# The written order of phase one of an mLSTM plus two MoE layers: gates earlier, R and the table switches moved, x copied at its transposes

## The chip, the cores and the metric

One core of a Trainium2 chip runs the whole program. The metric is the device time of one execution in microseconds (us). The kernel before takes 656.52 us, the median of three runs (656.23 to 657.03). Engines are called by the names that the profile uses: PE multiplies matrices, PEld loads their weights, DVE, ACT and POOL work on tiles elementwise, SP issues DMAs. Every engine takes its own instructions in the order in which they are written, and waits where an operand isn't there yet.

## What is computed

The input is an attention with gates (an mLSTM) for 2 batches, 8 heads, 768 positions and head size 40; its output x (1536 rows of 320) goes through a mixture of 4 experts and then through a gated layer of width 1536.

```python
m_new = maximum(f + m, i);  f_stab = exp(f + m - m_new);  i_stab = exp(i - m_new)
C = f_stab * C + i_stab * outer(v, k);   n = f_stab * n + i_stab * k
y[t] = sigmoid(o) * (C @ q) / maximum(abs(n @ q), 1)
# x: (1536, 320)
out += p[:, e] * (relu(x @ w1[e]) @ w2[e])        # e = 0..3
result = ((x2 @ w_a) * (x2 @ w_b)) @ w_out
```

## The kernel before

The attention is done in chunks of 128 positions: tile n is chunk j = n // 2 of batch n % 2, twelve tiles in all. In a chunk the product of q and k (`scores`, L411) is multiplied with a matrix of decays. That matrix is the exponential of a matmul of two tiles that the gates give: LT and Rr, the R of the title (`weights_of`, L402: PE, then ACT's exp, then a mask on POOL at L409). What comes before the chunk is held in a state cbd (`state`, L479).

Every matrix product with the experts' weights is done in two parts, a rounded high one and the rest: a weight piece is loaded by SP (L84), cast by ACT (wh, L88) and subtracted by POOL or DVE (wl, L90; `LOENG`, L34, says which engine). The same is done to x (`split_hi`, `split_lo`: xh by ACT at L130, xl by DVE at L133 and the rest of the third block by DVE at L135).

Phase one runs until 207 us. Its 72 **items** (`Item`, L203) are the first three half experts, 256 columns of x at a time: part a is 8 matmuls into psa (L201), a ReLU by ACT (hh, L218) and a subtraction by DVE (hl, L219), and part b, two items later, 6 matmuls into psy (L242 to L244). psa has two buffers, and so has psy in pairs. After items 7 and 11 of a round ACT or DVE takes psy away (`add_expert`, L251 and L253). Twelve items are a **round**; round r computes with the x of chunk r, and beside them runs the attention of chunk r + 1.

What of the attention stands where is written out by hand: `ev` (L622 to L650) is a list of (item, function, arguments), sorted by its first number, and the loop at L670 calls whatever is due before an item, in the middle of it (up to k + 0.5, between its part a and the part b that follows), and after it (up to k + 0.99). So the list is the order of every engine's queue. For chunks 2 to 5 the numbers are relative to the first item of the round (t0).

Names that the steps below touch: `gate1` to `gate4` and `gate_tail` (L331 to L393) go from a chunk's gates to LT (L368), zx (L367), exponentials and ET; `build_R` (L395) makes Rr from zx, on DVE for the first four tiles and on POOL afterwards; `split_qk` (L293) splits q and k (ACT L301, DVE L304); `s1b` (L423) multiplies scores and decays (DVE L425); `s2a` (L427) is the matmuls with v and with the state (PE L435, L441); `s2b` (L444) is seven small DVE steps from there to x (L451 to L464), closed by a copy by ACT of the last 64 columns of x (L465); `s3a` (L495) is three PE transposes of x, of which the third reads that copy; `s3b` splits their result. `table` (L525) makes ACT load the table of Exp or of Sigmoid, `o_gate` is the sigmoid (L315), `weights` (L528) the experts' weights pg, `weigh_k` (POOL L474) weighs k for the state. The tiles of PSUM that the attention uses (pt_...) come from one pool of four buffers, in the order in which they are asked for.

Of the kernel before, what the change touches and what calls it, by code (L numbers as in the profile page):

```python
# [7 lines left out]
F32 = mybir.dt.float32  # L8
# [5 lines left out]
AF = mybir.ActivationFunctionType  # L14
# [3 lines left out]
DM = H * D  # L18
# [12 lines left out]
NI = 12  # L31
NF = 2
NP = 4
LOENG = {0: "ppvppppp", 1: "pppppppp", 2: "pppppppp", 3: "vpvpvpvp", 4: "vpvpvpvp", 5: "vpvpvpvp"}  # L34
RB = 3
QB = 3
QENG = ("vector", "vector")
# [9 lines left out]
def mlstm_moe_kernel(ctx, tc, gates, qk, qc, kvo, dp, w1b, w2b, ident_d, bdmask_d, rsel_d, exp_d, out):  # L47
# [145 lines left out]
    def mm_group(ps, wh, wl, o0, c, o, n):  # L193
        k = lambda w, t: w[:, o0 + t * P:o0 + (t + 1) * P]
        x = lambda t, i: t[c][:, i, o:o + n]
        prs = [
            (k(wh, 0), x(xh, 0)), (k(wh, 1), x(xh, 1)), (k(wh, 2), x(xh, 2)), (k(wl, 0), x(xh, 0)),
            (k(wl, 1), x(xh, 1)), (k(wl, 2), x(xh, 2)), (k(wh, 0), x(xl, 0)), (k(wh, 1), x(xl, 1)),
        ]
        for i, (l, r) in enumerate(prs):  # L200
            nc.tensor.matmul(ps, l, r, start=(i == 0), stop=(i == len(prs) - 1))  # L201
# [59 lines left out]
    with ExitStack() as c1:  # L261
# [101 lines left out]
        def gate3(j):  # L363
            g = g_sb[j]
            zh, L, cm = g["zh"], g["L"], g["cm"]
            zx = a2.tile([64, P], F32R, tag="zx", name="zx")
            nc.vector.scalar_tensor_tensor(zx, zh[0:64].bitcast(F32), rsel[0:64, 16:17], L[0:64], op0=ALU.mult, op1=ALU.add)  # L367
            nc.vector.scalar_tensor_tensor(LT[j % 2][64:G], zh[64:G].bitcast(F32), rsel[64:G, 16:17], cm[64:G], op0=ALU.mult, op1=ALU.add)  # L368
            g["zx"] = zx

        def gate4(j):
# [72 lines left out]
        def s2b(n):  # L444
            j, b = n // 2, n % 2
            t = td[n]
            r = og[j][:, b].rearrange("p (h d) -> p h d", d=D)
            y = a2.tile([P, H, DE], F32, tag="y", name="y_t", bufs=1)
            pyv = t["py"][:, 0:H * DE].rearrange("p (h e) -> p h e", e=DE)
            if j > 0:  # L450
                nc.vector.tensor_tensor(  # L451
                    y, t["pi"][:, 0:H * DE].rearrange("p (h e) -> p h e", e=DE),
                    g_sb[j]["ET"][:, b * H:(b + 1) * H].unsqueeze(2).to_broadcast([P, H, DE]), op=ALU.mult)
                nc.vector.tensor_tensor(y, pyv, y, op=ALU.add)
            else:
                y = pyv
            dn = a2.tile([P, H, 1], F32, tag="dn", name="dn_t")
            nc.vector.tensor_scalar(dn, y[:, :, D:DE], -1.0, 1.0, op0=ALU.mult, op1=ALU.max)
            nc.vector.tensor_tensor(dn, y[:, :, D:DE], dn, op=ALU.max)
            nc.vector.reciprocal(dn, dn)  # L460
            x = a2.tile([P, DM + 64], F32, tag="x", name="x_t")
            xv = x[:, :DM].rearrange("p (h d) -> p h d", d=D)
            nc.vector.tensor_tensor(xv, y[:, :, 0:D], dn.to_broadcast([P, H, D]), op=ALU.mult)
            t["last"] = nc.vector.tensor_tensor(xv, xv, r, op=ALU.mult).ins  # L464
            nc.scalar.copy(x[:, DM:], x[:, 256:DM])  # L465
            t["x"] = x

        def weigh_k(n):
# [74 lines left out]
        load_kvo(1)  # L543
        load_qk(0, 0)
        load_qk(0, 1)
        load_qk(1, 0, nc.scalar)
        load_qk(1, 1, nc.scalar)
        for t in LT:
            nc.vector.memset(t[0:64].bitcast(F32), 1.0)
        nc.sync.dma_start(td[0]["kvo"][:, NK:NK + NV], kvo[0, :, NK:NK + NV])  # L550
        load_o(0, nc.sync)
        nc.sync.dma_start(td[1]["kvo"][:, NK:NK + NV], kvo[1, :, NK:NK + NV])
        nc.sync.dma_start(ident, ident_d)
        go(w0[:4])
# [30 lines left out]
        load_kvo(2)  # L585
        load_qk(3, 0)
        load_qk(3, 1)
        load_kvo(3)
        load_o(1, nc.sync)
        o_gate(0)  # L590
        for n in range(2):
            s1b(n, 0)
            s1b(n, 1)
        go(w0[:2])
        go(w0[:2])
        s2a(0, 0)
        s2a(0, 1)
# [15 lines left out]
        split_hi(td[1]["pv"], 0, P)  # L613
        split_lo(td[1]["pv"], 0, P)
        warm_up(1)
        go(w0[5:7])
        go(w0[4:7])
        gate1(1, V)
        load_gates(2)
        go(w1[2:6])  # L620

        ev = [  # L622
            (0.5, gate2, 1), (0.5, gate_hi, 1, nc.vector.tensor_copy), (0.5, table, AF.Exp), (0.6, go, w0[7:]), (0.7, go, w0[7:]), (0.8, go, w1[6:]), (0.9, gate_tail, 0), (0.95, weigh_k, 0),
            (1.5, gate3, 1), (1.5, build_R, 2, V, 0, 4), (1.5, weigh_k, 1), (1.6, gate4, 1), (1.8, go, w1[0:2]), (1.9, go, w1[0:2]), (1.9, state, 0),
            (2.5, build_R, 2, V, 4, 8), (2.5, state, 1), (2.7, go, w2[:2]), (2.8, gate_tail, 1), (2.8, go, w1[2:4]), (2.9, go, w1[2:4]), (2.9, scores, 2, 0),
            (3.5, scores, 2, 1), (3.5, build_R, 3, V, 0, 4), (3.8, go, w1[4:6]), (3.9, weights_of, 2, 0), (3.9, go, w1[4:6]), (3.9, go, w2[2:4]),
            (4.5, weights_of, 2, 1), (4.5, build_R, 3, V, 4, 8), (4.6, table, AF.Sigmoid), (4.7, go, w1[6:8]), (4.8, s1b, 2, 0), (4.8, go, w1[6:8]), (4.9, o_gate, 1), (4.9, go, w2[4:6]),
            (5.3, table, AF.Exp), (5.4, s1b, 2, 1), (5.5, s2a, 2, 0), (5.6, s2a, 2, 1), (5.8, go, w2[0:2]), (5.9, s2b, 2), (5.9, scores, 3, 0), (5.9, weights_of, 3, 0), (5.9, go, w2[6:8]), (5.9, go, w2[0:2]),
            (6.0, weigh_k, 2), (6.8, go, w2[2:4]), (6.9, s1b, 3, 0), (6.9, go, w2[2:4]),
            (7.0, scores, 3, 1), (7.0, weights_of, 3, 1), (7.2, weights), (7.4, s3a, 2), (7.5, weigh_k, 3), (7.7, go, w2[4:6]), (7.9, s1b, 3, 1), (7.9, s3b, 2), (7.9, go, w2[4:6]),  # L630
            (8.5, s2a, 3, 0), (8.6, s2a, 3, 1), (8.7, go, w2[6:8]), (8.9, s2b, 3), (8.9, go, w2[6:8]),
            (9.4, state, 2), (9.9, state, 3), (10.6, s3a, 3), (10.9, s3b, 3),
        ]
        for j in range(2, NCH):
            n0, n1, t0 = 2 * j, 2 * j + 1, NI * (j - 1)
            new = [
                (-6.4, load_kvo, n0), (-6.2, load_o, j, nc.sync), (-5.4, load_kvo, n1),
                (-4.4, load_qk, n0, 0), (-3.4, load_qk, n0, 1), (-2.4, load_qk, n1, 0), (-1.4, load_qk, n1, 1),
                (-8.4, gate1, j, V), (-5.8, gate2, j), (-5.1, gate_hi, j, nc.scalar.copy), (-3.6, gate3, j), (-3.4, gate4, j), (-3.1, build_R, n0, nc.gpsimd), (-2.0, build_R, n1, nc.gpsimd), (-1.1, gate_tail, j),
                (-1.5, split_qk, n0, 0), (-0.5, split_qk, n0, 1),  # L640
                (0.5, s1a, n0, 0), (1.5, s1a, n0, 1), (1.6, split_qk, n1, 0),
                (2.0, table, AF.Sigmoid), (2.4, s1b, n0, 0), (2.5, o_gate, j), (2.6, split_qk, n1, 1), (2.9, table, AF.Exp),
                (3.4, s1b, n0, 1), (3.5, s1a, n1, 0), (3.6, weigh_k, n0),
                (4.2, s2a, n0, 0), (4.5, s2a, n0, 1), (4.6, weigh_k, n1), (4.95, s2b, n0),
                (5.4, s1b, n1, 0), (6.2, s1a, n1, 1), (6.9, state, n0), (7.2, s3a, n0), (7.4, s1b, n1, 1), (7.6, state, n1), (7.9, s3b, n0),
                (8.2, s2a, n1, 0), (8.5, s2a, n1, 1), (8.95, s2b, n1), (10.6, s3a, n1), (10.9, s3b, n1),
            ]
# [188 lines left out]
```

## Time and profile before

| | us |
|---|---|
| time, median of 3 runs | 656.52 |
| the profiled execution: its time / its span | 656.55 / 654.8 |
| start, until the first item (0 to 19.25) | 19.25 |
| round 0 (19.25 to 71.85) | 52.60 |
| rounds 1, 2, 3 | 34.96, 34.95, 34.58 |
| round 4 | 31.15 |
| round 5 and all that follows (207.49 to the end) | 447.31 |
| busy over the span: PE, PEld, DVE, ACT, POOL | 630.3, 572.5, 429.3, 264.2, 181.3 |

The profile is of one execution whose own time is 656.55 us. A round is measured from the first matmul of its first item to that of the next round. "Busy" of PE is the time that the records of matmuls cover. Round 5 has no attention left beside it.

### The profile page before, as it was taken

Reading aid. Unit: us, or ns where it says so; the run is one execution under the profiler, and the core shown is the slowest. Engines: PE = TensorE matmul, PEld = TensorE weight load, DVE = VectorE, ACT = ScalarE, POOL = GpSimd, SP = SyncE. Lnnn points to the kernel's source line nnn. Section 1 sums busy time; section 2 is a strip of 40 time slices with the busy share of each in tenths; the row PEclk is TensorE's granted clock in tenths of the full one; section 3 lists DMA queues with packets and bytes.
Section 4 is the critical chain, followed back from the end, with each engine's and each line's share of the span. In section 5 each row is a group of like instructions: output and inputs, shape, how many; then the busy total and the mean of one; then the engine's idle time right before and its main releaser. Section 6 shows DMA issues by size and latency. Waiting matters only on the chain.

```text
span 654.8 us, 10289 instructions
## 1 busy us (share of the span) xinstructions
PE 630.3 (96%) x3798; PEld 572.5 (87%) x3799; DVE 429.3 (66%) x858; ACT 264.2 (40%) x592; POOL 181.3 (28%) x219
## 2 busy tenths in 40 slices
PE   8796999999899999999999999999999999999997
PEld 6686998989899988989888988898888888888886
DVE  7859687878665233433478888898765767764343
ACT  5563635445453322323343444354644433332221
POOL 3557351332310111233233333332121212220000
PEclk9799899999999999999999999999999999999999
DMA  7944216161600212222221222121111111000003
GB/s 217 253 144 107 61 54 163 55 163 55 155 12 23 68 45 59 74 62 72 80 69 52 72 66 69 52 69 53 35 36 34 53 34 52 18 0 2 1 10 111
DMA packets 27487, 45.99 MB, mean 70 GB/s; under 512 B 3189, under 2 KB 17773, under 8 KB 27437
## 3 DMA queue, kind: packets, MB, share of 16 engines
q1 hardware_dynamic: 27337, 45.00, 24.9%
q8 instruction: 30, 0.49, 0.3%
q10 hardware_dynamic: 100, 0.33, 0.2%
q14 instruction: 20, 0.16, 0.1%
HBM read 43.35 MB, written 1.97 MB: 69 GB/s over the span
## 4 chain that ended last, share of the span: by engine, by line
PE 80%; DVE 9%; ACT 4%; issue 4%; POOL 2%; DMA 1%; ACTq 0%; POOLq 0%; DVEq 0%
PE psa L201 33%; PE psy L242 11%; PE psy L244 10%; PE psy L243 10%; PE psb L201 10%; PE pt_y L435 1%; DVE LT L368 1%; ACT qs_t L301 1%; DMA acc<-in_w1b 1%; POOL wl L90 1%; PE pt_c L417 1%; DVE qs_t L304 1%; ACT L526 1%; ACT hh L218 1%; PE pt_i L441 1%
## 5 line engine op out<-in xcount | busy, mean ns | idle before, releaser
L242 PE MATMUL psy<-wh,hh 128*128 128x320 f32 x528 | 167.1, 317 | 9.2 <-ACT acc L251 9.1
L244 PE MATMUL psy<-wh,hl 128*128 128x320 f32 x528 | 163.7, 310 | 0.0
L243 PE MATMUL psy<-wl,hh 128*128 128x320 f32 x528 | 163.6, 310 | 0.0
L219 DVE SCALAR_TENSOR_TENSOR hl<-psa,hh 128x256 fp32r<-128x256 f32 (+1 forms) x132 | 71.9, 544 | 120.2 <-ACT hh L218 119.6
L201 PE MATMUL psa<-xh,wh 128*128 128x512 f32 (+1 forms) x504 | 122.5, 351 | 0.8 <-DVE xh L135 0.4
L218 ACT ACTIVATE hh<-psa 128x256 fp32r<-128x256 f32 (+1 forms) x132 | 62.8, 478 | 147.1 <-PE psa L201 147.1
L201 PE MATMUL psa<-xh,wl 128*128 128x512 f32 (+1 forms) x504 | 120.2, 347 | 0.0
L242 PEld LDWEIGHTS psy<-wh,hh 128*128 128x128 f32 x528 | 99.9, 189 | 16.3 <-ACT acc L251 10.2
L243 PEld LDWEIGHTS psy<-wl,hh 128*128 128x128 f32 x528 | 100.0, 189 | 4.0
L244 PEld LDWEIGHTS psy<-wh,hl 128*128 128x128 f32 x528 | 99.7, 189 | 0.0
L201 PEld LDWEIGHTS psa<-xh,wl 128*128 128x128 f32 x504 | 85.4, 190 | 12.6
L201 PEld LDWEIGHTS psa<-xh,wh 128*128 128x128 f32 x504 | 84.6, 190 | 9.0 <-DVE xh L135 0.9
L201 PE MATMUL psa<-xl,wh 128*128 128x512 f32 (+1 forms) x336 | 89.6, 348 | 0.0
L122 POOL TENSOR_TENSOR wl<-tp,lf 128x272 fp32r<-128x272 f32 x48 | 38.7, 807 | 124.3 <-DVE tp L121 124.3
L201 PEld LDWEIGHTS psa<-xl,wh 128*128 128x128 f32 x336 | 58.8, 190 | 8.2
L228 DVE TENSOR_TENSOR g<-psa,bs 128x512 f32<-128x512 f32 x36 | 24.9, 691 | 50.4 <-PE psa L201 50.4
L119 POOL TENSOR_TENSOR lf<-lf,sq 128x272 f32<-128x272 f32 x48 | 37.2, 775 | 70.3 <-ACT wh L118 39.5
L90 POOL TENSOR_TENSOR wl<-raw,wh 128x352 fp32r<-128x352 f32 x28 | 26.4, 950 | 96.9 <-ACT wh L88 84.3
L229 ACT CAST hh<-g 128x512 fp32r<-128x512 f32 x36 | 22.3, 620 | 72.4 <-DVE g L228 72.4
L409 POOL TENSOR_SCALAR_AFFINE_SELECT w_t<-w_t 128x512 f32<-128x512 f32 x24 | 15.2, 639 | 96.6 <-ACT w_t L408 90.6
L230 DVE TENSOR_TENSOR hl<-g,hh 128x512 fp32r<-128x512 f32 x36 | 24.9, 692 | 24.7 <-ACT hh L229 24.7
L224 ACT COPY bs<-psb 128x512 f32<-128x512 f32 x36 | 21.1, 587 | 44.0 <-PE psb L201 43.9
(118 smaller groups left out, 896.0 us busy)
## 6 DMA issues: line engine op xcount, KB each, us to landing
raw<-in_w2b SPq DMA_DIRECT2D x48, 272.0 KB, 2.7
qk_t<-in_qk SPq DMA_DIRECT2D x16, 480.0 KB, 6.3
raw<-in_w1b SPq DMA_DIRECT2D x40, 176.0 KB, 2.3
acc<-in_w1b SPq DMA_DIRECT2D x24, 176.0 KB, 3.6
kvo_t<-in_kvo SPq DMA_DIRECT2D x10, 364.5 KB, 4.4
og_t<-in_kvo SPq DMA_DIRECT2D x6, 320.0 KB, 3.0
out<-acc SPq DMA_DIRECT2D x12, 160.0 KB, 1.8
qc_t<-in_qc SPq DMA_DIRECT2D x10, 180.0 KB, 3.1
```

The source lines that it names most:

```text
L90: lo_eng.tensor_tensor(wl[:, cs], raw, wh[:, cs].bitcast(F32), op=ALU.subtract)
L119: nc.gpsimd.tensor_tensor(lf, lf, sq, op=ALU.mult)
L122: nc.gpsimd.tensor_tensor(wl[:, cs], tf, lf, op=ALU.add)
L201: nc.tensor.matmul(ps, l, r, start=(i == 0), stop=(i == len(prs) - 1))
L218: nc.scalar.activation(self.hh, ps, AF.Relu)
L219: nc.vector.scalar_tensor_tensor(self.hl, ps, 0.0, self.hh.bitcast(F32), op0=ALU.max, op1=ALU.subtract)
L228: nc.vector.tensor_tensor(g, ps, bs, op=ALU.mult)
L229: nc.scalar.copy(self.hh, g)
L230: nc.vector.tensor_tensor(self.hl, g, self.hh.bitcast(F32), op=ALU.subtract)
L242: nc.tensor.matmul(ps, lh, wh[:, off:off + DM], start=(fi == 0), stop=False)
L243: nc.tensor.matmul(ps, lh, wl[:, off:off + DM], start=False, stop=False)
L244: nc.tensor.matmul(ps, ll, wh[:, off:off + DM], start=False, stop=(fi == nf - 1))
```

## The change

The order of phase one is rewritten; nothing is computed otherwise.

- `gate1` to `gate4` and both `build_R` of chunks 3 to 5 stand 2 to 3.8 items sooner, so that `build_R` comes at items 6.25 and 8.0 of the round before instead of 8.9 and 10.0; those of chunk 2 are written out in the list of round 0, 1 to 2.8 items later than they were. In `gate3` LT is made ahead of zx.
- ACT's copy of x moves from the end of `s2b` to the start of `s3a`.
- Sigmoid, with its two table loads, moves from items 2.0 to 2.9 of a chunk's own round to items 8.0 to 9.5 of the round before.
- In round 0 the first two states and their `weigh_k` move from items 0.95 to 2.5 to items 2.5 to 5.45, `weights` from 7.2 to 3.2, and the pieces of the third half expert come up to 1.3 items sooner. Two more pieces of the first half expert are subtracted on DVE.
- The eight matmuls of part a take the products with the third block of x last.
- Loads: tile 1's q and k are issued by SP instead of ACT, the first two pieces ahead of o, tile 3's kvo in round 0; kvo has three buffers instead of four, and the second kvo of a chunk is loaded 3.4 items later, the next gates 2.3 items sooner.
- At the start the casts of the first two pieces stand ahead of the sigmoid.

The diff, without its unchanged lines:

```diff
-LOENG = {0: "ppvppppp", 1: "pppppppp", 2: "pppppppp", 3: "vpvpvpvp", 4: "vpvpvpvp", 5: "vpvpvpvp"}
+LOENG = {0: "ppvpvpvp", 1: "pppppppp", 2: "pppppppp", 3: "vpvpvpvp", 4: "vpvpvpvp", 5: "vpvpvpvp"}
...
-            (k(wh, 0), x(xh, 0)), (k(wh, 1), x(xh, 1)), (k(wh, 2), x(xh, 2)), (k(wl, 0), x(xh, 0)),
-            (k(wl, 1), x(xh, 1)), (k(wl, 2), x(xh, 2)), (k(wh, 0), x(xl, 0)), (k(wh, 1), x(xl, 1)),
+            (k(wh, 0), x(xh, 0)), (k(wh, 1), x(xh, 1)), (k(wl, 0), x(xh, 0)), (k(wl, 1), x(xh, 1)),
+            (k(wh, 0), x(xl, 0)), (k(wh, 1), x(xl, 1)), (k(wh, 2), x(xh, 2)), (k(wl, 2), x(xh, 2)),
...
-            t["kvo"] = a2.tile([P, NK + NV], F32, tag="kvo", name="kvo_t", bufs=4)
+            t["kvo"] = a2.tile([P, NK + NV], F32, tag="kvo", name="kvo_t", bufs=3)
...
+            nc.vector.scalar_tensor_tensor(LT[j % 2][64:G], zh[64:G].bitcast(F32), rsel[64:G, 16:17], cm[64:G], op0=ALU.mult, op1=ALU.add)
-            nc.vector.scalar_tensor_tensor(LT[j % 2][64:G], zh[64:G].bitcast(F32), rsel[64:G, 16:17], cm[64:G], op0=ALU.mult, op1=ALU.add)
...
-            nc.scalar.copy(x[:, DM:], x[:, 256:DM])
...
+            nc.scalar.copy(x[:, DM:], x[:, 256:DM])
...
-        load_qk(1, 0, nc.scalar)
-        load_qk(1, 1, nc.scalar)
+        load_qk(1, 0)
+        load_qk(1, 1)
+        nc.sync.dma_start(td[1]["kvo"][:, NK:NK + NV], kvo[1, :, NK:NK + NV])
+        go(w0[:2])
-        nc.sync.dma_start(td[1]["kvo"][:, NK:NK + NV], kvo[1, :, NK:NK + NV])
-        go(w0[:4])
+        go(w0[2:4])
...
-        load_kvo(3)
+        go(w0[:2])
-        go(w0[:2])
...
+        go(w0[4:5])
-        go(w0[4:7])
+        go(w0[5:6])
-            (0.5, gate2, 1), (0.5, gate_hi, 1, nc.vector.tensor_copy), (0.5, table, AF.Exp), (0.6, go, w0[7:]), (0.7, go, w0[7:]), (0.8, go, w1[6:]), (0.9, gate_tail, 0), (0.95, weigh_k, 0),
-            (1.5, gate3, 1), (1.5, build_R, 2, V, 0, 4), (1.5, weigh_k, 1), (1.6, gate4, 1), (1.8, go, w1[0:2]), (1.9, go, w1[0:2]), (1.9, state, 0),
-            (2.5, build_R, 2, V, 4, 8), (2.5, state, 1), (2.7, go, w2[:2]), (2.8, gate_tail, 1), (2.8, go, w1[2:4]), (2.9, go, w1[2:4]), (2.9, scores, 2, 0),
-            (3.5, scores, 2, 1), (3.5, build_R, 3, V, 0, 4), (3.8, go, w1[4:6]), (3.9, weights_of, 2, 0), (3.9, go, w1[4:6]), (3.9, go, w2[2:4]),
+            (0.5, gate2, 1), (0.5, gate_hi, 1, nc.vector.tensor_copy), (0.5, table, AF.Exp), (0.6, go, w0[7:]), (0.7, go, w0[6:]), (0.8, go, w1[6:]), (0.9, gate_tail, 0),
+            (1.5, gate3, 1), (1.5, build_R, 2, V, 0, 4), (1.6, gate4, 1), (1.8, go, w1[0:2]), (1.9, go, w1[0:2]),
+            (2.5, build_R, 2, V, 4, 8), (2.5, weigh_k, 0), (2.7, go, w2[:2]), (2.8, gate_tail, 1), (2.8, go, w1[2:4]), (2.9, go, w1[2:4]), (2.9, scores, 2, 0),
+            (3.0, weigh_k, 1), (3.2, weights), (3.5, scores, 2, 1), (3.5, build_R, 3, V, 0, 4), (3.8, go, w1[4:6]), (3.9, weights_of, 2, 0), (3.9, go, w1[4:6]), (3.9, go, w2[2:4]),
-            (5.3, table, AF.Exp), (5.4, s1b, 2, 1), (5.5, s2a, 2, 0), (5.6, s2a, 2, 1), (5.8, go, w2[0:2]), (5.9, s2b, 2), (5.9, scores, 3, 0), (5.9, weights_of, 3, 0), (5.9, go, w2[6:8]), (5.9, go, w2[0:2]),
-            (6.0, weigh_k, 2), (6.8, go, w2[2:4]), (6.9, s1b, 3, 0), (6.9, go, w2[2:4]),
-            (7.0, scores, 3, 1), (7.0, weights_of, 3, 1), (7.2, weights), (7.4, s3a, 2), (7.5, weigh_k, 3), (7.7, go, w2[4:6]), (7.9, s1b, 3, 1), (7.9, s3b, 2), (7.9, go, w2[4:6]),
-            (8.5, s2a, 3, 0), (8.6, s2a, 3, 1), (8.7, go, w2[6:8]), (8.9, s2b, 3), (8.9, go, w2[6:8]),
-            (9.4, state, 2), (9.9, state, 3), (10.6, s3a, 3), (10.9, s3b, 3),
+            (5.0, state, 0), (5.2, go, w2[0:2]), (5.3, table, AF.Exp), (5.4, s1b, 2, 1), (5.4, go, w2[0:2]), (5.45, state, 1), (5.45, load_kvo, 3), (5.5, s2a, 2, 0), (5.6, s2a, 2, 1), (5.9, s2b, 2), (5.9, scores, 3, 0), (5.9, weights_of, 3, 0), (5.9, go, w2[6:8]), (5.95, go, w2[2:4]),
+            (6.0, weigh_k, 2), (6.1, go, w2[2:4]), (6.4, gate1, 2, V), (6.6, go, w2[4:6]), (6.8, go, w2[4:6]), (6.9, s1b, 3, 0),
+            (7.0, scores, 3, 1), (7.0, weights_of, 3, 1), (7.4, s3a, 2), (7.4, go, w2[6:8]), (7.45, gate2, 2), (7.5, weigh_k, 3), (7.6, go, w2[6:8]), (7.9, s1b, 3, 1), (7.9, s3b, 2),
+            (8.3, gate_hi, 2, nc.scalar.copy), (8.5, s2a, 3, 0), (8.6, s2a, 3, 1), (8.9, s2b, 3),
+            (9.4, state, 2), (9.5, gate3, 2), (9.9, state, 3), (10.0, build_R, 4, nc.gpsimd), (10.2, gate4, 2), (10.6, s3a, 3), (10.9, s3b, 3), (10.9, gate_tail, 2), (11.0, build_R, 5, nc.gpsimd),
-                (-6.4, load_kvo, n0), (-6.2, load_o, j, nc.sync), (-5.4, load_kvo, n1),
+                (-6.4, load_kvo, n0), (-6.2, load_o, j, nc.sync), (-2.0, load_kvo, n1),
-                (-8.4, gate1, j, V), (-5.8, gate2, j), (-5.1, gate_hi, j, nc.scalar.copy), (-3.6, gate3, j), (-3.4, gate4, j), (-3.1, build_R, n0, nc.gpsimd), (-2.0, build_R, n1, nc.gpsimd), (-1.1, gate_tail, j),
+                (-4.0, table, AF.Sigmoid), (-3.5, o_gate, j), (-2.5, table, AF.Exp),
-                (2.0, table, AF.Sigmoid), (2.4, s1b, n0, 0), (2.5, o_gate, j), (2.6, split_qk, n1, 1), (2.9, table, AF.Exp),
+                (2.4, s1b, n0, 0), (2.6, split_qk, n1, 1),
+            if j > 2:
+                new += [
+                    (-11.4, gate1, j, V), (-8.4, gate2, j), (-7.7, gate_hi, j, nc.scalar.copy), (-7.4, gate3, j), (-6.0, gate4, j),
+                    (-5.75, build_R, n0, nc.gpsimd), (-4.0, build_R, n1, nc.gpsimd), (-1.1, gate_tail, j),
+                ]
-                new += [(0.1, load_gates, j + 1)]
+                new += [(-2.2, load_gates, j + 1)]
```

## Rows read from the trace of the kernel before

**Rows 1.** Stages: length, busy us of PE, PEld, DVE, ACT, POOL, clock, DMA, GB/s.
```profile
19.25:71.85 52.60, 42.37 (x281) 40.19 (x282) 39.28 (x71) 25.49 (x63) 32.89 (x36) 0.87 0.55 150
71.85:106.81 34.96, 33.10 (x259) 32.40 (x259) 27.30 (x55) 16.23 (x39) 11.81 (x13) 1.00 0.34 90
...
207.49:654.80 447.31, 442.69 (x2426) 394.56 (x2424) 274.25 (x544) 162.14 (x365) 102.36 (x124) 1.00 0.18 50
```

**Rows 2.** PE's waits over the whole run: total us, times, longest us.
```profile
PE psy L242 <- ACT acc L251: 9.1, 4, 4.4
PE pt_u L486 <- POOL kw_t L474: 3.3, 1, 3.3
PE pt_y L435 <- DVE w_t L425: 3.0, 6, 1.0
...
PE pt_y L435 <- ACT warm L526: 0.6, 1, 0.6
PE psb L201 <- DVE xh L135: 0.6, 1, 0.6
```

**Rows 3.** The two stretches after PE's long waits, columns as in rows 1.
```profile
25.48:30.90 5.42, 5.42 (x25) 5.42 (x26) 5.29 (x10) 1.00 (x3) 2.63 (x4) 0.50 0.91 251
...
64.72:72.00 7.28, 7.28 (x31) 6.95 (x32) 4.98 (x9) 3.67 (x8) 5.33 (x4) 0.53 0.26 69
```

**Rows 4.** Timeline around 24 us: start, us, engine, line, out<-in, [idle before <-releaser].
```profile
22.89 0.42 DVE L219 SCALAR_TENSOR_TENSOR hl<-psa,hh 128x256 fp32r<-128x256 f32 x1
23.94 0.31 ACT L375 ACTIVATE ex<-L 64x128 f32<-64x128 f32 x1
...
25.48 1.58 PE L486 MATMUL pt_u<-kvo_t,kw_t 128*120 128x123 f32 x6 [3.27 <-POOL kw_t L474]
```

**Rows 5.** Timeline around 60 us.
```profile
56.34 4.58 DVE L368 SCALAR_TENSOR_TENSOR LT<-zh,rsel,cm 48x128 fp32r<-48x128 f32 x1
62.02 0.17 DVE L458 TENSOR_SCALAR dn_t<-y_t 128x8 f32<-128x8 f32 x1
63.72 0.24 ACT L465 COPY x_t<-x_t 128x64 f32<-128x64 f32 x1 [8.83 <-DVE x_t L464]
64.72 0.41 PE L242 MATMUL psy<-wh,hh 128*128 128x320 f32 x1 [4.42 <-ACT acc L251]
```

**Rows 6.** Timeline of ACT and PE at the end of round 2, items 9 to 11.
```profile
137.04 0.94 ACT L251 ACTIVATE acc<-psy,pg 128x320 f32<-128x320 f32 x2
137.86 0.39 ACT L218 ACTIVATE hh<-psa 128x256 fp32r<-128x256 f32 x1
138.13 1.06 ACT L301 CAST qs_t<-qk_t 120x1024 fp32r<-120x1024 f32 x1
139.14 0.48 ACT L130 CAST xh<-pt_x 128x384 fp32r<-128x384 f32 x1
...
133.84 0.40 PE L201 MATMUL psa<-xl,wh 128*128 128x256 f32 x2
...
135.68 0.40 PE L201 MATMUL psa<-xl,wh 128*128 128x256 f32 x2
137.62 0.41 PE L242 MATMUL psy<-wh,hh 128*128 128x320 f32 x1 [1.54 <-ACT acc L251]
```

**Rows 7.** Timeline of ACT in round 3: a table load and the next ReLU.
```profile
150.60 1.28 ACT L526 ACT_TABLE_LOAD   x1
...
152.00 0.36 ACT L218 ACTIVATE hh<-psa 128x256 fp32r<-128x256 f32 x1
```

**Rows 8.** Timeline of DVE and POOL at the end of round 1: R beside s2b.
```profile
98.39 0.50 DVE L451 TENSOR_TENSOR y_t<-pt_i,ET 128x328 f32<-128x328 f32 x1
...
99.46 0.69 DVE L458 TENSOR_SCALAR dn_t<-y_t 128x8 f32<-128x8 f32 x1
...
96.32 3.79 POOL L398 TENSOR_TENSOR Rr<-zx,rsel 64x1024 fp32r<-64x1024 f32 x2
```

**Rows 9.** A group of round 0 by line: count, busy us, mean ns, idle before.
```profile
L90 POOL TENSOR_TENSOR wl<-acc,wh 128x352 fp32r<-128x352 f32 x20 | 19.5, 994 | 6.4 <-ACT wh L88 6.4
```

## The prediction

> **What bounds the kernel now.** I read the stages first. From 207.49 us on PE is busy 442.69 of 447.31 us, and the change reaches that part only through the order of eight matmuls. Round 1 takes 34.96 us with PE busy all but 2, and rounds 2 to 4 are no longer. Round 0 does the same kind of work in 52.60 us [rows 1]: that is the stage to look at.
>
> The second view is what PE waits for [rows 2]. Three lines carry it. 9.1 us go to L251, which takes psy away; 3.3 us to the weighed k of the first state; 3.0 and 0.6 us to `s2a`, whose decays come late. They sum to 16.0 us.
>
> The third view is PE's clock. After the wait of 3.27 us [rows 4] PE works 5.42 us at 0.50, and after the one of 4.42 us [rows 5] 7.28 us at 0.53 [rows 3]; otherwise it is at full speed in phase one. At half speed half of the time is lost: 5.42 x 0.5 = 2.7 us and 7.28 x (1 - 0.53) = 3.4 us. So waits and clock together cost 16.0 + 6.1 = 22.1 us, and that is nearly all that a better order can bring.
>
> **Part by part, what is removed.**
>
> *The first states.* PE reaches `state(0)` 3.27 us before POOL has weighed k [rows 4]. At item 5 k is long weighed. The wait goes, and the half clock behind it: 3.3 + 2.7 = 6.0 us.
>
> *The copy of x, and LT.* L465 waits in ACT's queue for the end of `s2b` on DVE: 8.83 us in round 0. The ReLU and L251, whose inputs were there, stand behind it, and PE stands behind L251 for 4.42 us [rows 5]. In rounds 1 to 3 it is the same at some 1.5 us each (1.54 in round 2 [rows 6]; all four together 9.1 [rows 2]). In round 0 DVE is late because LT, a step on 48 x 128 elements, took 4.58 us [rows 5], beside POOL at work; with LT ahead of zx, R can't start before it. At `s3a` x is ready, so these waits go: 9.1 + 3.4 = 12.5 us.
>
> *Sigmoid.* The two table loads of 1.28 us [rows 7] stand, in a chunk's own round, ahead of ReLUs on which the decays' last product (L425) waits. That and the late masks of round 0 make the 3.0 + 0.6 us at `s2a` [rows 2]. Away from there the wait goes: 3.6 us.
>
> **What is added.**
>
> *The copy at the transposes.* Now the third transpose waits for a copy that is issued right before it, behind whatever ACT holds. For the first tile of a chunk `s3a` stands in the middle of an item, directly behind part a, so ACT has that item's ReLU (0.36 [rows 7]) and the copy (0.24 [rows 5]) to do, and PE the two other transposes, about 0.2: with the handoffs 0.5 us of waiting, once a round, 2.0 us in rounds 1 to 4. Below, it is nothing if ACT is ahead; above, a cast of 1.06 [rows 6] in the way makes it 1.6 a round. For the second tile, in the three rounds 1 to 3, `split_qk`'s cast (1.06) stands ahead too. In round 2 the cast ended where L130 began, 139.14 [rows 6].
>
> *The Exp table at item 9.5.* It now stands right ahead of L251. Take round 2. Part a of item 9 ended at 134.2, that of item 10 at 136.1 [rows 6]. With ACT free the ReLU of item 9 begins at 134.3 and the table load at 134.7; from the start of a load to the next ReLU it takes 1.40 us [rows 7], so L251 begins at 136.1 and its first copy ends at 136.6. PE is there at 135.9 (the start of its last two, 135.68, and 0.2): 0.74 us instead of 1.54. Then ReLU 136.9, cast 137.2 to 138.2, copy to 138.45; the third transpose can start at 138.5 and was due at 137.75: another 0.75. So PE waits 1.49 us where it waited 1.54, in each of three rounds: 2.2 + 2.25 = 4.5 us. Bounds: nothing if ACT gets there early, and double if one more cast of 1.06 is late.
>
> With the 2.0 us of the first tiles this is 6.5 us, against 4.7 us at L251 (9.1 less 4.4 [rows 2]) and, by my split of the 3.0, 1.5 us at `s2a` that these rounds lose today: **rounds 1 to 4 gain nothing.**
>
> The Trainium skill, "TensorE: Matmul & The Clock Gate", Architectural detail, says that ACT and DVE are strict first in, first out, and that of PE's queue only weight loads are pulled ahead. That speaks against this part of the change. If PE could run part b past the waiting transpose, the sum would be some 4 us lower, by the transposes' terms; nothing in these rows shows it doing so.
>
> *R and the gates earlier.* Per round, nothing is added. R on POOL (3.79 us for two [rows 8]) slows DVE steps whose inputs all lie in SBUF: L458 takes 0.69 us beside it, 0.17 alone [rows 5, 8]. L451, which reads PSUM, takes its 0.50 beside it. At item 6.25 DVE has hl, L425 and the state's product to do, all of PSUM; at 8.0 R should be over before `s2b`. If it isn't, 0.5 us of DVE per step, covered by the items until `s3a` at 10.6: 0. The Trainium skill, "SBUF — State Buffer", Who interferes with whom, has this as a rule: a DVE instruction with two SBUF inputs and a POOL one that reads SBUF exclude each other. By it, the two pieces moved to DVE in round 0 could each wait for one of POOL's, 0.99 us [rows 9], and the sum would be 2 us higher if none of that were covered.
>
> *Round 0's new waits.* PE's gap no longer hides DVE. hl of item 0 ends at 23.3, after gate1 [rows 4], while PE would want its buffer at 22.2; an added piece on DVE and less of POOL beside gate1 cancel: 0.5 us by my count, 0 to 1.1. `gate_tail(1)` wants ACT's exponentials, which began at 23.94 [rows 4] and have a table load, a cast and two ReLUs ahead: 0.9. The two states now ask for PSUM buffers that `s1b` of tile 2 must free, behind POOL's masks, and these behind pieces of 0.99 us each [rows 9]: 1.6 (0 to 3). `s3a` of tile 2: 0.6 for the copy, and its buffer waits for another `s1b`: 0.5 to 2.2 in all, and I take 1.0, near the lower end, since the longest wait of PE for L425 today is 1.0 [rows 2]. `s3a` of tile 3, behind exponentials and the cast: 1.3. Sum 5.3, of which 0.3 comes back as the third block's products come last (0.4 us of PE's wait at the first item was for L135): **5.0**, with 1 and 11 as ends.
>
> *The rest.* Third block last in the later phase: half of the 0.6 us at psb [rows 2], -0.3. The casts ahead of the first sigmoid give POOL its first pieces sooner, and o's DMA comes later; x of tile 0 has its sigmoid at about the same time: 0, within 0.5. Tile 1's q and k go through SP about 1 us later, with the decays' chain ahead of their use: 0. kvo with three buffers, and the loads that stand behind it on SP: each waits for a state that PE does at least two items earlier: 0. Moving tile 3's kvo out of a stretch with DMA at 0.91 [rows 3] brings the pieces behind it forward; nothing waits on them once POOL is the later one: 0. `weights` at 3.2: four DVE steps in the shadow of PE: 0.
>
> **The sum**, against the profiled execution's 656.55 us, which is within 0.03 of the median: 656.55 - 22.1 + 5.0 + 6.5 - 0.3 = 645.65, **645.7 us**. By its own terms this case spans 641 to 650 (round 0's added waits 1 to 9).
>
> **Rivals.**
>
> *ACT is never in the way.* If ACT keeps ahead at item 9.5 and at the transposes, 6.5 us and 1.9 of round 0's fall away: 637.3, 634 to 640. For it: ACT is busy only 16.2 of 35 us in a round [rows 1]. Against: in-order queues, and the casts right there.
>
> *The waits of round 0 meet.* If POOL's masks and the states come one behind the other in one wait of over 3 us, the clock falls as it did after 3.27 us [rows 3, 4] and takes some 3 us more: 645.7 + 3 + 3 = 652. For it: POOL has 32.9 us of work in round 0 [rows 1], which must now fit in some 41. It decides from 3 us in one piece; waits of 1.5 us did no harm.
>
> *ACT is the new bound: slower.* The place is items 9 to 11. If at each copy the whole queue lies ahead (L251 twice 0.94, ReLU, cast 1.06, table 1.4, copy 0.24: 4.0 us against my 1.5), four rounds lose 10 us more, and the five copies behind an exponential of 0.6 us more, 3: 645.7 + 13 = 659. It decides from 10.9 us beyond my added 11.5. For it: one L465 holds ACT for 8.83 us today [rows 5]. Against: ACT's inputs are ready this time.
>
> *It does nothing.* All that goes comes back in the same rounds: 656. For it: in rounds 1 to 4 that is my own reckoning; but the two long waits of round 0 have no successor of that length.
>
> **How the numbers follow.** My forecast has 0.56, ACT out of the way 0.18, the meeting waits 0.17, slower 0.06, nothing 0.03. The first three are all faster by more than 0.2%, 1.3 us, which is about what a measurement of this kernel can tell from no change: faster 0.91, within 0.2% 0.03, slower 0.06. The range takes in the first three: 635 to 652.
>
> **What would show it.** Right: round 0 is 41 to 43 us long, with the clock at 1.00 and no wait of PE over 2 us; L465 disappears from ACT's waits; LT takes 0.35 us everywhere; the third transpose waits for ACT in every chunk; PE still waits for L251 by 0.5 to 1 us in rounds 1 to 3, whose lengths stay within 0.5 us of before. Wrong: rounds 1 to 3 at 33 us (ACT was ahead), a stretch at half clock (the waits met), or a PE wait on SP's loads, which I have costed at nothing.

## The result and the profile after

The changed kernel takes 647.60 us (median of 4, 646.99 to 648.15) beside 656.77 for the kernel before in the same comparison: a ratio of 0.9848, 95% interval 0.9811 to 0.9886. Its profiled execution takes 647.9 us with a span of 646.2, that of before 656.55 and 654.8.

The stages of after, by the first matmul of each round as in [rows 1] and in its columns: start, rounds 0, 1 and 4, and the rest.

```profile
0.00:18.11 18.11, 15.70 (x90) 11.21 (x91) 14.85 (x38) 11.84 (x22) 8.34 (x17) 1.00 0.81 232
18.11:64.77 46.66, 38.64 (x282) 36.78 (x282) 37.82 (x72) 28.91 (x68) 32.26 (x34) 0.93 0.66 184
64.77:99.50 34.73, 33.26 (x259) 32.23 (x258) 24.46 (x55) 17.04 (x39) 12.17 (x13) 1.00 0.32 79
...
168.09:199.12 31.03, 30.64 (x241) 30.08 (x240) 19.14 (x44) 11.96 (x27) 3.02 (x4) 1.00 0.14 39
199.12:646.20 447.08, 442.75 (x2426) 394.53 (x2424) 274.34 (x544) 162.28 (x365) 102.83 (x124) 1.00 0.17 50
```

One boundary of before has to be put right for the comparison. Its round 4 begins at 175.90 us and not at 176.34, which is the third matmul of that item, so its rounds 3 and 4 take 34.14 and 31.59 us and not 34.58 and 31.15. PE of before, and the two stages:

```profile
175.90 0.40 PE L201 MATMUL psa<-xh,wh 128*128 128x256 f32 x2
...
176.34 0.39 PE L201 MATMUL psa<-xh,wh 128*128 128x256 f32 x1
...
141.76:175.90 34.14, 32.16 (x254) 31.61 (x253) 26.09 (x54) 16.75 (x38) 11.58 (x12) 1.00 0.39 103
175.90:207.49 31.59, 31.05 (x240) 30.30 (x239) 19.78 (x46) 14.83 (x32) 2.54 (x4) 1.00 0.14 37
```

Against the kernel before the start is 1.14 us shorter, round 0 5.94, rounds 1 to 4 0.23, 0.22, 0.28 and 0.56, the rest 0.23: 8.6 us in all. So round 0 carries the gain, as forecast, but it is 46.66 us long where I expected 41 to 43, and its clock is 0.93.

PE's waits of after, columns as in [rows 2]:

```profile
PE pt_x L140 <- ACT x_t L496: 4.7, 9, 1.2
PE pt_e L389 <- POOL eb L380: 2.8, 1, 2.8
PE psy L242 <- ACT acc L251: 1.7, 3, 0.6
...
PE psa L201 <- DVE hl L219: 1.3, 1, 1.3
PE pt_y L435 <- DVE w_t L425: 1.3, 1, 1.3
PE pt_y L435 <- issue: 1.0, 1, 1.0
PE psb L201 <- DVE xh L135: 0.6, 1, 0.6
```

L251 fell from 9.1 to 1.7 us, and the wait for the weighed k is gone. New are the third transpose (L140) and one that I hadn't foreseen, 2.8 us for eb. The timeline around it, POOL and then PE, and three stretches in the columns of [rows 1], the first two within the wait and the third with the work behind it:

```profile
57.10 2.35 POOL L398 TENSOR_TENSOR Rr<-zx,rsel 64x1024 fp32r<-64x1024 f32 x1
59.41 0.63 POOL L380 TENSOR_TENSOR eb<-expd,ex 16x2 f32<-16x2 f32 x1
...
56.88 0.33 PE L140 MATMUL pt_x<-ident,x_t 128*128 128x128 f32 x1 [1.21 <-ACT x_t L496]
57.04 0.25 PE L386 MATMUL pt_e<-ident,ex 96*128 96x96 f32 x1
60.09 1.15 PE L389 MATMUL pt_e<-eb,expd 16*120 16x2 f32 x5 [2.81 <-POOL eb L380]
...
57.50:58.00 0.50, 0.00 (x0) 0.00 (x0) 0.49 (x2) 0.22 (x1) 0.50 (x1) 0.81 0.00 0
58.00:59.00 1.00, 0.00 (x0) 0.00 (x0) 1.00 (x1) 0.00 (x0) 1.00 (x1) 0.50 0.00 0
57.50:65.00 7.50, 4.91 (x22) 4.89 (x23) 3.63 (x6) 1.84 (x5) 4.40 (x3) 0.54 0.48 115
```

eb is a product on 16 x 2 elements that `gate4` of chunk 2 makes on POOL. The change puts `gate4` at 10.2, behind `build_R` of tile 4 at 10.0: eb stands behind 2.35 us of R on POOL, and PE stands behind eb. After it PE does 4.91 us of work at a granted clock of 0.54, most of it at the lower of its two levels (1.2 and not 2.4 GHz), which loses 4.91 x 0.46 = 2.3 us. Wait and clock make 5.1 us. But the clock is already down before 58.0, early in the wait, and PE had waited 1.21 us at L140 just before: whose the half clock is, the wait for eb alone can't say (e4 below).

### The profile page after: what moved, and what is told of

Its sections match the earlier page's. It is cut to its first block, busy times and chain, and to the rows that moved or that the text cites. A ratio compares the mean times of both kernels' runs of the same rounds, so it can differ in the third digit from the quotient of the medians.

```text
span 646.2 us, 10283 instructions
## 1 busy us (share of the span) xinstructions
PE 626.6 (97%) x3798; PEld 568.6 (88%) x3799; DVE 419.9 (65%) x860; ACT 267.2 (41%) x592; POOL 182.6 (28%) x217
## 4 chain that ended last, share of the span: by engine, by line
PE 90%; DVE 5%; ACT 2%; issue 1%; POOL 1%; DVEq 0%; ACTq 0%; POOLq 0%
PE psa L201 37%; PE psy L242 12%; PE psy L244 11%; PE psy L243 11%; PE psb L201 10%; PE pt_y L435 3%; PE pt_c L417 2%; PE pt_i L441 1%; PE pt_a L407 1%; PE pt_u L485 1%; PE pt_e L389 1%; PE pt_x L140 1%; ACT hh L218 0%; ACT qs_t L301 0%; ACT acc L251 0%
## 5 line engine op out<-in xcount | busy, mean ns | idle before, releaser
L201 PE MATMUL psa<-xh,wh 128*128 128x512 f32 (+1 forms) x504 | 149.6, 351 | 1.7 <-DVE hl L219 1.3
L201 PE MATMUL psa<-xh,wl 128*128 128x512 f32 (+1 forms) x504 | 147.1, 346 | 0.0
L201 PEld LDWEIGHTS psa<-xh,wl 128*128 128x128 f32 x504 | 90.2, 189 | 12.6
L201 PEld LDWEIGHTS psa<-xh,wh 128*128 128x128 f32 x504 | 89.1, 189 | 9.6 <-DVE hl L219 1.5
L409 POOL TENSOR_SCALAR_AFFINE_SELECT w_t<-w_t 128x512 f32<-128x512 f32 x24 | 17.9, 752 | 83.0 <-ACT w_t L408 56.0
```

## The experiments

A common mark for lengths of rounds is the first row of L253, by which DVE takes a round's last psy. "End of 0" is its start in the first round, the next columns are the distances to the next ones; "first item" is the start of the first item's first matmul. All are from profiled executions. The medians of e1 to e12 are beside 655.9 to 656.4 for the kernel before.

| | edit | median (range) us | first item | end of 0 | 1 | 2 | 3 |
|---|---|---|---|---|---|---|---|
| before | | | 19.25 | 76.67 | 34.91 | 34.97 | 34.46 |
| after | | 647.60 (646.99-648.15) | 18.11 | 69.55 | 34.73 | 34.73 | 33.87 |
| e1 | before + copy | 660.65 (655.59-662.73) | 21.17 | 74.53 | 38.17 | 37.17 | 34.93 |
| e2 | before + states | 656.71 (654.57-657.65) | 18.62 | 75.06 | 35.08 | 36.56 | 34.36 |
| e3 | before + LT | 657.96 (654.54-662.05) | 19.16 | 75.41 | 38.16 | 38.22 | 34.61 |
| e5 | before + all three | 659.70 (655.01-661.92) | 20.64 | 70.50 | 38.15 | 37.67 | 34.56 |
| e12 | e5 + one load | 648.83 (646.67-650.05) | 18.78 | 67.88 | 34.63 | 34.64 | 33.75 |
| e4 | after, eb ahead of R | 645.20 (644.75-646.42) | 18.13 | 68.22 | 34.74 | 34.75 | 33.85 |
| e6 | after, two pieces back on POOL | 648.68 (648.14-649.76) | 18.09 | 70.01 | 34.72 | 34.73 | 33.84 |
| e7 | after, states back | 651.64 (650.94-651.87) | 18.11 | 73.52 | 34.72 | 34.73 | 33.87 |
| e8 | after, copy back | 651.60 (649.67-655.92) | 18.09 | 72.92 | 34.71 | 34.91 | 33.79 |
| e9 | after, gates and R back | 649.21 (647.49-649.81) | 18.10 | 70.01 | 34.71 | 34.71 | 33.17 |
| e10 | after, Sigmoid back | 648.53 (647.39-649.15) | 18.11 | 69.78 | 34.56 | 34.55 | 33.69 |
| e11 | after, three edits | 637.98 (637.77-638.11) | 18.10 | 67.00 | 32.58 | 32.56 | 31.68 |

**One part alone, on the kernel before (e1 to e3).** e1 moves the copy:

```diff
         def s2b(n):
...
-            nc.scalar.copy(x[:, DM:], x[:, 256:DM])
...
         def s3a(n):
...
+            nc.scalar.copy(x[:, DM:], x[:, 256:DM])
```

> The kernel before with one edit: ACT's copy of the last columns of x moves from the end of s2b to the start of s3a. My theory: the four waits at L251 go (9.1 us before), but in round 0 LT still takes 4.58 us of DVE, so x is late at the transposes instead: PE waits there for some 3 us in one piece and the clock still falls to half behind it. Rounds 1 to 3 gain some 0.4 us each. Sum: 653 to 655, from 656.5. Rival: the copy alone carries the gain that I gave to 'the copy and LT', 12.5 us less the 4.7 of new waits at the transposes: about 649.

It is slower, ratio 1.0061 (1.0036 to 1.0086). Neither account has that. L251 is gone from the waits, but the third transpose waits 10.9 us (9 times, up to 2.5), and the profiled execution has half clock behind such waits in rounds 1 and 2, which are 3 and 2 us longer. The total hides a gain: from the first item to the end of round 0 e1 takes 53.4 us and before 57.4. The first item itself is 1.9 us late, as PE waits 2.0 us for tile 1's q and k at the start, which this edit doesn't touch: so much of the profiled execution's 4.2 us isn't shown to be the edit's.

e2 moves `weigh_k` and `state` of tiles 0 and 1, as the change does.

> The kernel before with one edit: in round 0 weigh_k of the first two states moves from items 0.95 and 1.5 to 2.5 and 3.0, the states from 1.9 and 2.5 to 5.0 and 5.45. My theory: the wait of 3.3 us and the half clock behind it (2.7 us) go, 1 us of new waits comes: about 651.5, with the clock at 1.00 where 25.5 to 30.9 had 0.50. Rival: DVE and ACT are late there anyway, PE meets another wait of 2 to 3 us in its place and the clock falls again: 654 to 656.

The rival is right in kind: 656.71, 0.9991 (0.9969 to 1.0012). The wait of 3.3 us goes and another of 2.89 comes; POOL, then DVE and PE of e2:

```profile
33.75 1.90 POOL L90 TENSOR_TENSOR wl<-acc,wh 128x352 fp32r<-128x352 f32 x2
35.60 0.69 POOL L409 TENSOR_SCALAR_AFFINE_SELECT w_t<-w_t 128x512 f32<-128x512 f32 x1
...
36.76 0.67 DVE L425 TENSOR_TENSOR w_t<-pt_c,w_t 128x512 f32<-128x512 f32 x1
...
37.53 0.31 PE L435 MATMUL pt_y<-kvo_t,w_t 128*128 128x82 f32 x1 [2.89 <-issue]
```

A mask (L409) stands behind two pieces on POOL, L425 behind the mask, `s2a` behind L425. From 39.0 to 42.5 PE works at a clock of 0.54 again.

e3 swaps LT and zx.

> The kernel before with one edit: in gate3 LT is made ahead of zx, so that R on POOL, which reads zx, can't start before LT is done. My theory: LT takes 0.35 us instead of 4.58 in round 0, DVE reaches x some 2 us sooner or more, the wait of 4.42 us at L251 shrinks to about 2, and the clock behind it stays up or falls for a shorter time: 651 to 654; rounds 1 to 3 unchanged. Rival: R then lies on the small steps of s2b instead (0.5 us more for each of them) and x is as late as before: 656.

1.0029 (1.0002 to 1.0057): no gain. In round 0 LT takes 0.83 us and not 4.58 [rows 5], L251's longest wait is 3.1 us and not 4.4, and PE is at half clock behind it all the same. As the rival says, R now lies on two steps of `s2b` (L458 takes 1.08 us and L459 0.72), and L465 comes 1.3 us sooner than in before, at 62.42. In the profiled execution, the slowest of the twelve, the clock fell in rounds 1 and 2 too.

**The three together, and what was missing (e5, e12).**

> The kernel before with the three edits of the first runs together: the copy of x at s3a, the first two states and weigh_k later, LT ahead of zx. Alone they gave +4, 0 and +1.5 us. My theory now: they stand in series, each alone uncovers the next late thing, so together they gain: the 4.4 us at L251 and the half clock behind it go, while the 2.9 us of the run with the states alone (L425 behind a mask that POOL does late, behind two subtractions of weight pieces) stay, with their half clock: 650 to 653. Rival: the parts simply add, 656 or more. Second rival: these three carry the whole gain, 647 to 649.

Only the first rival stands: 1.0044 (1.0020 to 1.0067). The table says where: the end of round 0 comes 6.2 us sooner, and rounds 1 and 2 give 5.9 of it back. The end of round 1 in e5, first SP, then ACT and PE, and the waits of SP's queue:

```profile
92.18 0.34 SPq L324 DMA_DIRECT2D qc_t<-in_qc  x1
92.63 8.33 SPq L291 DMA_DIRECT2D qk_t<-in_qk  x4
...
98.10 1.04 ACT L301 CAST qs_t<-qk_t 120x1024 fp32r<-120x1024 f32 x1 [1.86 <-DMA qk_t<-in_qk]
99.05 0.24 ACT L496 COPY x_t<-x_t 128x64 f32<-128x64 f32 x1
...
99.34 0.33 PE L140 MATMUL pt_x<-ident,x_t 128*128 128x128 f32 x1 [2.26 <-ACT x_t L496]
...
SPq L324 <- PE pt_i L441: 93.8, 8, 15.1
```

`load_kvo` issues two DMAs, and the second (L324), into qc with its two buffers, waits until PE has used the old qc in `s2a` (L441). The loads of q and k for the next chunk stand behind it on SP, are issued from 92.63 on and land after the cast wants them. The cast waits 1.86 us, the copy of x stands behind the cast, PE behind the copy. SP stands as long in the kernel before (85.8 us in 8 waits), and there no cast waits for q and k: ACT reached it later, behind the L251 that L465 held up [rows 6]. In round 2 it began 5.2 us after the first of these loads was issued, at 132.89, where e5's ACT was free for it 3.6 us after. So the late load cost nothing. e12 adds to e5:

```diff
-                (-6.4, load_kvo, n0), (-6.2, load_o, j, nc.sync), (-5.4, load_kvo, n1),
+                (-6.4, load_kvo, n0), (-6.2, load_o, j, nc.sync), (-2.0, load_kvo, n1),
```

> The kernel before with the three edits of the run before (copy of x at s3a, first two states later, LT ahead of zx; 659.7 together) and one more: in the rounds the load of a chunk's second kvo stands 3.4 items later (item -2.0 instead of -5.4), behind three of the four loads of q and k. My theory: SP waits at that kvo's qc until s2a of the tile before has read the old one, q and k stand behind it and land late, the cast of split_qk waits for them 0.7 to 1.9 us at the end of a round, and with the copy of x behind the cast on ACT this now reaches PE at the third transpose. With the load moved the cast waits for no DMA, the second transposes wait 0.5 to 1.2 us instead of up to 2.3, the clock stays up in rounds 1 and 2, which take 35 us instead of 38: 652 to 655. Rival: it is R and the gates, or the sigmoid, at their old places that make x late; rounds 1 and 2 stay over 37 us: 658 to 660.

648.83, 10.9 us less than e5, in the direction of my theory and beyond its numbers; 0.9895 (0.9877 to 0.9913). Of the 10.0 us between the two profiled executions 7.4 lie in rounds 1 to 3, where the edit acts; the other 2.6 are there by the end of round 0. Of these, 1.9 were there at the first item, since e5's execution waited 1.4 us for tile 1's q and k at the start and e12's, by the same code, didn't; and in round 0 e5's had a stretch at half clock and e12's none. The same place in e12:

```profile
77.54 1.34 SPq L291 DMA_DIRECT2D qk_t<-in_qk  x3
78.93 0.40 SPq L322 DMA_DIRECT2D kvo_t<-in_kvo  x1
89.56 0.33 SPq L324 DMA_DIRECT2D qc_t<-in_qc  x1
...
93.52 1.04 ACT L301 CAST qs_t<-qk_t 120x1024 fp32r<-120x1024 f32 x1
94.45 0.25 ACT L496 COPY x_t<-x_t 128x64 f32<-128x64 f32 x1
...
94.75 0.33 PE L140 MATMUL pt_x<-ident,x_t 128*128 128x128 f32 x1 [0.30 <-ACT x_t L496]
```

Three of the four loads are issued 12 us before qc's, the cast doesn't wait, PE waits 0.30 us. SP still waits 83.8 us for qc's buffer, but q and k are ahead of it. Four edits of the kernel before thus come to within 1.2 us of the whole change, by the medians.

**One part undone (e6 to e10).** e7 puts `weigh_k` and the states back, e8 the copy, e6 the old LOENG of piece set 0, e9 gates and R of chunks 3 to 5, e10 the Sigmoid.

> The kernel after with one edit undone: weigh_k and the states of the first two tiles at their old places (items 0.95 to 2.5). My theory: PE waits 2 to 3.3 us for the weighed k again and works some 5 us at half clock, against some 1 us of later waits that go: 650 to 652. Rival (time only moved, as the states alone gained nothing on the kernel before): 647 to 648.

> The kernel after with one edit undone: the copy of x closes s2b again. My theory: 4.7 us of waits at the transposes go, waits at L251 of some 1 us in each of four rounds come: 646 to 649. Rival one: L251 waits 9 us as before and the clock falls behind them, 652 or more. Rival two: the copy's move is a loss by itself, as alone on the kernel before (+4 us), and its undoing gains 3 us or more: 645 or less.

e7 is as expected: +4.0 us, the wait of 3.2 us is back, and PE works from 24.5 to 28.0 at a clock of 0.53. e8 too costs 4.0, more than my account and less than the first rival. In the profiled execution, 3.0 us longer than that of after, all of it is in round 0: L251 waits 5.9 us over the run, but rounds 1 to 3 are as long as in after. So the copy at `s3a` is worth 3 to 4 us in round 0 (4.1 in e1) and nothing later. In e8 it isn't L251 that brings them, which waits 0.8 us in round 0, but a wait of 2.57 us at `s2a` with half clock behind it. L465 had held ACT for 4.1 us shortly before; that this made the decays late is read from the order of the queues and not tested.

```profile
40.55 0.24 ACT L465 COPY x_t<-x_t 128x64 f32<-128x64 f32 x1 [4.11 <-DVE x_t L464]
...
47.55 1.42 PE L435 MATMUL pt_y<-kvo_t,w_t 128*128 128x82 f32 x8 [2.57 <-issue]
...
47.50:54.50 7.00, 6.78 (x31) 6.42 (x32) 4.51 (x9) 2.10 (x6) 3.20 (x4) 0.55 0.26 59
```

> The kernel after with one edit undone: the two pieces of the first half expert that went to DVE are subtracted on POOL again. I had costed these at nothing. My theory now: without them POOL's masks of tile 2 come late, as in the run with the states alone, and PE waits 2 to 3 us in one piece for L425 with some 2 us of half clock behind it: 650 to 652. Rival, the account on record: cancels, 647 to 648.

> The kernel after with one edit undone: gates and both R of chunks 3 to 5 at their old places in rounds 1 to 3 (R at items 8.9 and 10.0 instead of 6.25 and 8.0). The account on record costs this move at nothing: 647 to 648. My theory now: R lies beside the steps of s2b again, whose inputs are in SBUF, x comes later, the third transpose of the second tile waits 1.5 us or more, and in some of the executions the clock falls behind such a wait as it did in the runs with the copy alone: 648 to 652, with a spread of several us between executions.

> The kernel after with one edit undone: Sigmoid with its two table loads in a chunk's own round again (items 2.0 to 2.9) instead of items 8.0 to 9.5 of the round before. My account on record: L251's waits of 0.56 us in three rounds and most of the 0.5 us behind them at the second transposes go, waits of some 0.36 us at L425 return in four rounds: 645.5 to 648. Rival (the move is what keeps PE's waits in rounds 1 to 3 short): waits of 1 us or more return at L425 or L251, and the time is 650 or more.

Each is about 1 us slower by the medians (1.1, 1.6, 0.9), with intervals that overlap that of after (0.9880 with 0.9857 to 0.9903, 0.9887 with 0.9865 to 0.9909, 0.9876 with 0.9854 to 0.9898). After was measured in another comparison, so none of the three can be told from no effect. e6's wait of 2 to 3 us didn't come; what shortens e2's 2.89 us in after wasn't settled. In e9 x is late as expected (L138 waits 2.7 us in three), but L251's waits go for it. The move of the loads, the third buffer of kvo and the new start were not undone.

**Taking away what is left (e4, e11).** e4:

```diff
-(9.9, state, 3), (10.0, build_R, 4, nc.gpsimd), (10.2, gate4, 2),
+(9.9, state, 3), (10.2, gate4, 2), (10.3, build_R, 4, nc.gpsimd),
```

> The kernel after with one edit: build_R of tile 4 at item 10.3 instead of 10.0, so that it stands behind gate4's product eb on POOL's queue (10.2) and not ahead of it. My theory: the 2.8 us that PE waits for eb at the end of round 0 go, and with them the half clock behind it (4.7 us of work at 0.5, so 2.3 us): about 643 where after has 647.6, with the clock at 1.00 up to the end of round 0. Rival: PE still meets waits there (the transposes of x wait for ACT, 1.2 us, right before) and the clock falls anyway: about 645, or, if R of tile 4 is then late for item 12, 647.

645.20: 2.4 us, the wait and not the clock; the first rival is right. PE waits 0.5 us for eb where it waited 2.8, but the 1.2 us at L140 right before stay and the clock falls. So of the 5.1 us that follow eb in after only the wait is shown to be eb's. The stretch and DVE of e4:

```profile
57.50:65.00 7.50, 7.25 (x33) 7.14 (x34) 7.11 (x8) 2.43 (x7) 3.91 (x3) 0.54 0.25 60
...
56.67 5.28 DVE L304 TENSOR_TENSOR qs_t<-qk_t,qs_t 40x512 fp32r<-40x512 f32 x2 [0.50 <-ACT qs_t L301]
```

e11 adds two edits to e4: the Exp table at item 8.6, right behind the Sigmoid, and the copy as a step `x_copy` of its own.

```diff
-                (-4.0, table, AF.Sigmoid), (-3.5, o_gate, j), (-2.5, table, AF.Exp),
+                (-4.0, table, AF.Sigmoid), (-3.5, o_gate, j), (-3.4, table, AF.Exp),
...
-(6.9, state, n0), (7.2, s3a, n0),
+(6.9, state, n0), (6.95, x_copy, n0), (7.2, s3a, n0),
...
-(8.95, s2b, n1), (10.6, s3a, n1),
+(8.95, s2b, n1), (9.95, x_copy, n1), (10.6, s3a, n1),
```

> The kernel after with three edits: R of tile 4 behind eb on POOL (645.2 alone); the copy of x as a step of its own at items 6.95 and 9.95, ahead of the ReLU and the cast of the item that has the transposes; the Exp table right behind the sigmoid (item 8.6) instead of item 9.5. My theory: the waits at the third transpose (4.7 us) and at L251 (1.7) go, 1 to 2 us of other waits come, and with the 1.2 us ahead of eb gone the clock stays up at the end of round 0 (3.4 us): 637 to 641. Rival one: ACT's queue is only reordered, what follows is late by as much: 644 to 646. Rival two: the waits go but the clock falls all the same: 641 to 643.

637.98, ratio 0.9717 (0.9691 to 0.9742): faster than both kernels. No L140 and no L251 is left among PE's waits. From 64 to 200 us PE of e11, in the columns of [rows 1]:

```profile
64.00:200.00 136.00, 136.00 (x1073) 134.99 (x1073) 96.04 (x216) 66.91 (x148) 41.24 (x44) 1.00 0.35 90
```

Rounds 1 to 3 are 2.2 us shorter each. The waits' rows of after named some 1.5 of that (0.52, 0.56, 0.39); the other 0.7 lie in PE's busy time, 33.26 us in round 1 of after and 32.58 here, and why isn't shown. PE still waits 1.8 us for eb in round 0, with no wait at L140 ahead of it, and the clock stays up. The table's and the copy's edit were not run singly.

## Why the prediction was right, and where it was not

The time is 2.25 us above the sum. By stages: round 0 lost 5.9 us and not 10.9 (+5.0), the start 1.1 and not 0 (-1.1), rounds 1 to 4 lost 1.3 where I had 0.3 more (-1.6), the rest 0.23 for my 0.3. So the prediction is right in where the gain lies and in which waits go, and it is this near to the time by errors that cancel, which is luck.

- **Round 0 and the two long waits: right.** They and their clock are gone (waits above, against [rows 2]). Undone in after, the states cost 4.0 us where I had 6.0: the half clock behind the wait was 3.5 us long and not 5.42 [rows 3].
- **"The copy of x, and LT", 12.5 us, with the loads at 0: the step that failed.** I gave the gain to these two edits. Alone they gain nothing in total (e1, e3); in round 0 the copy gains 4.1 us in e1 and 3.4 in e8, and e3 takes 56.3 us from the first item to the end of round 0 where before takes 57.4. The sum holds only with the edit that I costed at nothing, "the loads that stand behind it on SP: 0". The zero is right for the whole change, but its reason is wrong: I had looked at kvo's buffer, which a state frees, and not at that of qc, which `s2a` frees later, nor at q and k behind it. The copy's move makes their lateness PE's. On top of the three parts that one number is worth 10.9 us by the medians, of which the profiled executions show 7.4 in rounds 1 to 3 (e5, e12).
- **Round 0's new waits, 5.0: near in total, one missing.** Rows of after: 1.3 at hl (0.5 in the sum), 1.0 and 1.3 at `s2a` (1.6 as the states'), 0.4 and 1.2 at L140 (1.0 and 1.3): 5.2. The 0.9 for `gate_tail(1)` didn't come, so here too errors cancel. But gate4's own instruction eb, behind R on POOL, is in no term: 2.8 us of wait, and 2.3 of clock that e4 shows to fall without it, 5.1 for the 5.0 that round 0 missed. I had costed the gates' move by what R does to DVE, and not by what it puts R ahead of on POOL.
- **The rival "the waits of round 0 meet" came in part**, at another place. Its condition, 3 us in one piece, is wrong: in after the clock was down behind 1.2 us of wait, a transpose and the first part of the next wait, and in e4 behind 1.2 and 0.5 us.
- **Rounds 1 to 4 gain nothing: right within 0.3 us in rounds 1 to 3; 0.56 in round 4.** L251 waits 0.56 us (0.74 in the sum), the first transposes 0.52 (0.5), the second 0.39 (0.75):

```profile
92.81 1.28 ACT L526 ACT_TABLE_LOAD   x1
94.10 0.20 ACT L526 ACTIVATE warm<-rmask 1x1 f32<-1x1 f32 x1
94.21 0.91 ACT L251 ACTIVATE acc<-psy,pg 128x320 f32<-128x320 f32 x2
...
94.77 0.41 PE L242 MATMUL psy<-wh,hh 128*128 128x320 f32 x1 [0.56 <-ACT acc L251]
```

- **Sigmoid, 3.6 us.** Undone in after (e10), L251's waits go, L425 waits 2.7 us in five where after has 1.3 in one, and the time is 0.9 us longer, not told from none: what the move takes away at `s2a` it gives back at L251, as in my sum for rounds 1 to 4.
- **The rival "ACT is never in the way", 637.3**, is what e11 makes true in rounds 1 to 3, at 638.0. Its last two edits are worth 7.2 us on top of e4 where I had priced the rival at 8.4. That the totals lie 0.7 apart is in part luck, since the sum under the rival knew nothing of eb.
- **Third block last and the other edits.** psb still waits 0.6 us for L135, so of the 0.3 nothing came from there; the rest is 0.23 shorter all the same. In round 4 of before the third matmul, at 176.34, started some 0.2 us after it was due, behind L135; now it stands seventh. LT takes 2.4 us for all six (407 ns each). The start was not undone, but the column "first item" shows it: 18.09 to 18.13 us in all eight kernels with the new start, 18.62 to 21.17 in the six with the old one, the two latest being e1 and e5, whose PE waits 2.0 and 1.4 us for tile 1's q and k there. Which of the start's edits does this isn't shown.

## What to carry to other kernels

When an edit frees a queue, list what had been late behind the blockage without anyone noticing, and compare the landing of each load with the new time of its use: here the freed queue alone made rounds 1 to 3 5.9 us longer, and a load that the same change moves was worth 10.9 us once three parts were in. When a step is moved, follow each of its instructions on each engine: the smallest one (16 x 2 elements) stood behind the largest. Test parts by undoing them from the whole as well as alone, and compare stage by stage: e1's total hid a gain of 4.1 us in round 0 under losses elsewhere.

## What was not expected of the hardware

The length of one wait doesn't say whether the clock falls. Behind the 1.84 us at L140 in e5's round 2 the granted clock was 0.62 from 137 to 141 us; in e12 PE waited 2.86 us at `s2a` and 2.06 at a transpose in round 0, and in that execution the clock stayed at full speed:

```profile
137.00:141.00 4.00, 3.96 (x20) 3.81 (x21) 2.14 (x5) 1.47 (x5) 0.00 (x0) 0.62 0.70 171
...
20.00:40.00 20.00, 15.05 (x117) 14.20 (x116) 17.20 (x29) 13.51 (x32) 13.86 (x16) 1.00 0.77 215
40.00:60.00 20.00, 17.53 (x142) 16.96 (x140) 15.60 (x34) 9.23 (x23) 13.92 (x16) 1.00 0.57 148
```

Kernels with waits of up to 1.7 to 2.5 us in rounds 1 to 3 spread over 7 us between executions (e1, e3, e5), the kernel before, with 1.5, over 6.4 in 29, and e11 over 0.3. The mean granted clock goes with it: in e3 it was 0.991 in the execution of 654.54 us and 0.978 in that of 662.05. The Trainium skill, "TensorE: Matmul & The Clock Gate", Part 1, calls the number of matmuls that one kernel runs at the lower clock run-variable; these spreads agree. So such waits want a chance of half clock in their price, and not the threshold that I used.

Two L304 of DVE took 5.28 us beside R in e4, against some 0.75 each over the run of after; both of their inputs lie in SBUF. The Trainium skill, "SBUF — State Buffer", Who interferes with whom, has a DVE step with two SBUF inputs and a POOL step that reads SBUF contend for one shared read interface, and this agrees: an R that is moved holds up whatever DVE step stands at its new place.
